# Loading q with four tokens to a partition, and its decay always at the cast, in a retention and Wave-MLP kernel

## The chip, the cores and the metric

The kernel runs on one core of one Trainium2 chip. The metric is the device time of one execution in microseconds (us), the median of several runs.

## What is computed

Inputs q, k and v are float32 of 4 batches, 8 heads, 768 tokens and 64 features. Each head h has a decay gamma_h = 1 - 2^(-5-h). The first stage is a linear recurrence over tokens t:

```python
state = gamma * state + outer(k[t], v[t])          # 64 x 64, for each batch and head
y[t]  = (1 / 8) * q[t] @ state
```

Its output, with the heads side by side, is x (4 x 768 x 512). The second stage is

```python
theta = x @ w_theta
yr = w_tok_r @ (x * cos(theta))                    # over tokens
yi = w_tok_i @ (x * sin(theta))
u = x + yr + yi
out = u + relu(u @ w_ch)                           # float32
```

## The kernel before

**Units.** The recurrence is cut into 24 units: 4 batches, 3 blocks of 256 tokens, 2 halves of 4 heads; unit n has half n mod 2. A unit loads 256 KB each of q, k and v. A partition holds two neighbouring tokens of 4 heads, so a load (`load_unit`, tokens `Lq`, `Lk`, `Lv`) is 128 partitions x 4 heads in rows of 2 x 64 floats, 512 bytes each. `kqf` tiles (16 buffers) take k and q, `vf` tiles (9) take v.

The decay over tokens is factored: v is multiplied by gamma^-t at its cast to bfloat16 (`cv`, table `vsc`), and q by gamma^t / 8. For q there are two ways, chosen unit by unit: either at the cast (`cqs`, table `qsc`), with a plain copy of the unit's output later (`XB`), or a plain cast (`cq`), and then the output, which has q's token in the free dimension, is multiplied by the table `qx` when it is copied out of PSUM (`XA`, DVE alone). `qx` is 128 x 4 x 768 floats, made by eight exponentials on ACT (`const8`, `const9`) from the positions that `constA` makes on POOL.

Then for a unit: `ck` casts k; `Tk`, `Tq` transpose k and q on PE and `E` copies them to `kqT` (or `Dk` does it by a DMA transpose on SP); `ST` adds k x v to the state in PSUM, `S0`, `S1` keep it in float32 and `SB` copies it in bfloat16 to block-diagonal tiles; `A` makes the scores `at_ps` and `m` multiplies them by the causal mask; `I` (state) and `Y` (scores x v) give the unit's output in PSUM; `XA` or `XB` copies it to `xT`, where the tokens lie in order.

**Chunks.** 128 tokens with all heads are a chunk C (24 in all, 6 to a batch). `Tx` and `Ex` (or `Dx`, a DMA transpose) give x; `Hh` is x @ w_theta, `CN` its sine and cosine on ACT, `z` the product with x. `M.t.s` adds chunk s of the batch to output tile t with both token matrices; `u` adds x; `Tu`, `Eu` (or `Du`) transpose u; `O` is u @ w_ch; `f` applies relu and adds u, into one of 4 `ot` buffers; `SO` stores. `Mh`, `uh` and so on are the last tile in halves. `Pth`, `Pch`, `Pw` load the weights by POOL's queue; `Tw`, `Ew` transpose the token matrices; `Z` are products of zeros on PE, written to no output.

**Order.** A list, `ORDER`, written out by hand or by a planner, gives one sequence of tokens; each engine executes its own instructions in that order. A letter at the end of a token names the engine or queue: p POOL (GpSimd), v DVE (VectorE), a ACT (ScalarE), s SP's DMA queue. So a load with an `a` stands in ACT's stream between its copies. DMAs of SP and ACT use eight semaphores in turn.

Of the kernel before, what the change touches and what calls it, by code (L numbers as in the profile page):

```python
# [25 lines left out]
Tk.1 E.1.a Y.0 ST.1 XB.0.1.a cqs.2.v Z.34 S0.1.v S1.1 cv.2.p SB.1.0.a Pth Lq.3.s Z.18 XB.0.0.v Tq.2  # L26
A.1 SB.1.1.a ck.2.a Tk.2 const7 I.1 Z.23 m.1 Y.1 XB.1.0.a Lk.3.s E.2.v XB.1.1.v A.2 ck.3.p m.2 ST.2
S0.2.v S1.2 SB.2.1.a Z.11 cqs.3.p Tq.3 Lv.3.s Tx.0 Tk.3 Z.3 ck.4.p Lv.4.s Lk.5.s Lq.5.s Lv.5.s
Lq.6.s Lk.6.s Lv.6.s Lq.7.s E.3.a SB.2.0.v I.2 Y.2 XB.2.1.a Ex.0.a cv.3.v cq.4.p Tk.4 Lq.8.s A.3
ST.3 Lk.7.s S0.3.v SB.3.0.a S1.3 Lv.7.s Lk.8.s Tx.1 Tq.4 SB.3.1.p cv.4.p m.3 Pw.1.0 XB.2.0.a Ex.1.a  # L30
I.3 Lv.8.s cq.5.a Y.3 E.4.a Pw.0.0 ST.4 Hh.0 ck.5.a cv.5.v CN.0.1 A.4 CN.0.0 S0.4.v Tq.5 Hh.1 Tk.5
XB.3.0.v SB.4.0.p XB.3.1.v SB.4.1.a Pw.0.1 Hh.2 m.4 E.5.v I.4 Y.4 ST.5 ck.6.a Tk.6 Tx.2 cq.6.a
CN.1.1 CN.1.0 XA.4.1 A.5 XA.4.0 m.5 Lq.9.s Ex.2.v S0.5.v z.0.p Tq.6 E.6.a CN.2.0 cv.6.p Hh.3
SB.5.0.v Tx.3 Tw.1.0 z.1.v SB.5.1.a Ew.1.0.v Ex.3.a CN.2.1 A.6 I.5 Y.5 ST.6 XA.5.0 z.2.v Tw.0.0
CN.3.0 Tx.4 CN.3.1 Ew.0.0.v S0.6.v XA.5.1 Ex.4.v Hh.4 CN.4.0 CN.4.1 Tw.0.1 M.0.1 Pw.1.1 z.3.v M.0.0
Tw.0.2 Pw.1.2 Ew.0.2.a SB.6.1.a Hh.5 z.4.p SB.6.0.p Lk.9.a M.0.3 ck.7.p cqs.7.p M.0.2 CN.5.1 CN.5.0
cq.8.a m.6 Ew.0.1.v Tw.1.1 Tw.1.2 Ew.1.1.v Lv.9.s M.0.4 M.1.0 Tx.5 Ew.1.2.v M.1.1 S1.6 Tk.7 M.1.4
Pch Ex.5.v cv.7.p z.5.v Tq.8 Tq.7 M.1.2 M.0.5 I.6 Y.6 ST.7 E.7.v ck.8.a A.7 u.0 S0.7.v m.7 XA.6.1
SB.7.1.a M.1.5 M.1.3 XA.6.0 Tw.1.3 M.2.5 Pw.0.2 M.2.3 u.1 S1.7 Tk.8 M.2.1 M.2.0 SB.7.0.v Ew.1.3.a
Tu.0 I.7 cv.8.p E.8.a cv.9.p Y.7 ST.8 A.8 cqs.9.v ck.9.v M.2.4 Du.1 Lk.10.s Eu.0.a XB.7.1.a XB.7.0.v  # L40
S0.8.v SB.8.0.v M.2.2 Tx.6 Tq.9 Tk.9 Lv.10.a cv.10.p ck.10.p Lq.10.s S1.8 u.2 m.8 O.0 E.9.a SB.8.1.a
Hh.6 Tw.1.4 I.8 Y.8 A.9 CN.6.0 Du.2 Lq.14.s CN.6.1 Ex.6.v f.0 ST.9 Tw.0.3 Hh.7 Ew.1.4.v Ew.0.3.a
S0.9.v Tw.0.4 M.3.0 Tw.1.5 CN.7.0 CN.7.1 M.3.2 Dx.7 M.3.1 M.3.5 M.3.3 Lv.12.s Lk.12.s Ew.1.5.v
XA.8.1 Ew.0.4.v Lq.12.s M.3.4 u.3 S1.9 Tw.0.5 Tk.10 M.4.5 cqs.10.p XA.8.0 m.9 M.4.3 Tq.10 SB.9.1.a
SB.9.0.a I.9 O.2 Lq.11.s Lk.11.s E.10.a Lk.15.s Ew.0.5.v Lk.14.s Y.9 ST.10 A.10 z.7.p Lv.11.s
# [24 lines left out]
u.12 A.20 Dk.21 XA.19.1 S0.20.v XA.19.0 ck.22.a cq.22.a SB.20.1.p cv.22.p M.14.3 M.14.5 M.14.1  # L70
M.14.4 M.14.2 M.14.0 SB.20.0.p u.13 m.20 S1.20 Hh.19 I.20 Y.20 SO.10.s Lq.23.s Lk.23.s cv.21.v u.14
A.21 ST.21 CN.19.0 CN.19.1 S0.21.v M.15.3 M.15.5 S1.21 m.21 XA.20.1 Hh.18 CN.18.1 CN.18.0 Dx.18
Dk.22 ck.23.a M.15.4 M.15.2 SB.21.0.p M.15.1 M.15.0 SB.21.1.v Lv.23.s Du.12 Dx.19 XA.20.0 O.9 f.9
I.21 Y.21 A.22 ST.22 M.16.1 cqs.23.p u.15 m.22 S0.22.v z.18.p z.19.p M.16.5 SB.22.0.p M.16.4 O.12
M.16.0 SO.8.a M.16.2 M.16.3 SB.22.1.p XB.21.0.a XB.21.1.a SO.11.s Du.14 cv.23.p Dk.23 f.12 Du.13
Dx.20 Dx.21 Hh.21 u.16 I.22 A.23 Y.22 ST.23 CN.21.0 CN.21.1 Hh.20 CN.20.1 S0.23.v XA.22.1 XA.22.0
SB.23.0.a M.17.1 M.17.3 CN.20.0 M.17.0 SB.23.1.p I.23 M.17.2 m.23 Y.23 O.13 M.17.4 z.21.v M.17.5
Mh.0.1 Mh.0.3 XB.23.1.v f.13 Hh.23 u.17 XB.23.0.a SO.13.a CN.23.1 Du.16 Hh.22 z.20.v CN.22.1 Mh.0.2
M.19.3 Dx.23 CN.23.0 Dx.22 Mh.0.0 M.21.1 M.19.1 z.23.p CN.22.0 SO.6.a Du.17 M.18.1 O.16 M.21.2
M.19.2 M.19.0 M.18.3 f.16 SO.9.a M.18.5 z.22.p M.18.2 O.17 M.19.4 M.18.0 Mh.0.4 M.18.4 f.17 u.18  # L80
Du.15 SO.12.s O.15 M.19.5 f.15 u.19 SO.16.s M.22.2 M.22.1 O.14 Mh.1.3 SO.15.a Mh.0.5 uh.0 f.14
M.22.0 M.21.5 M.22.3 M.22.5 Du.19 M.21.4 SO.17.s M.22.4 Du.18 M.21.0 O.19 Mh.1.0 Mh.1.2 M.21.3
M.20.2 Mh.1.4 u.22 O.18 f.19 M.20.0 M.20.1 Tuh.0 u.21 Du.22 Du.21 f.18 M.20.3 Euh.0 M.20.4 Mh.1.1
M.20.5 u.20 O.22 Mh.1.5 uh.1 f.22 Tu.20 SO.14.a SO.19.s Eu.20.a O.21 SO.18.a Tuh.1 Euh.1 f.21 O.20
f.20 Oh.0 Oh.1 SO.21.a SO.22.s SO.20.s fh.1 SOh.1 fh.0 SOh.0 Z.31
# [14 lines left out]
def kernel(  # L100
# [53 lines left out]
    def load_unit(name, src, n, e):  # L154
        b, i, h = unit(n)
        t = io.tile([P, HU, 2, D], FT, name="vf" if name == "vf" else "kqf", bufs=9 if name == "vf" else 16)
        queues[e].dma_start(
            out=t.rearrange("p h a d -> p h (a d)"),
            in_=src[b, h * HU:(h + 1) * HU, i * 2 * P:(i + 1) * 2 * P, :].rearrange(
                "h (p a) d -> p h (a d)", a=2))  # L160
        raw[name, n] = t
# [3 lines left out]

    def Lq(n, e):
        load_unit("qf", q, n, e)
# [35 lines left out]
    def const2():  # L203
# [4 lines left out]
        for h in range(H):  # L208
# [6 lines left out]
        nc.gpsimd.memset(K["zerob"], 0.0)  # L215
        arg = const.tile([P, nI * 2, H], FT, name="arg")
        nc.vector.tensor_mul(arg, _bcast_last(posn.rearrange("p i a -> p (i a)"), H),
                             _bcast_mid(lg, nI * 2))
# [415 lines left out]
```

## Time and profile before

| | |
|---|---|
| runs | median 168.77 us of 3 (168.33 to 169.25) |
| profiled execution | 168.7 us, span 166.9 us, granted PE clock 0.999 |
| busy, share of span | PE 92%, DVE 68%, ACT 47%, POOL 46% |
| DMA | 34.93 MB in 69,062 packets, mean 209 GB/s |
| first real transpose on PE | 7.46 us |
| scores (A) of units 0 to 5 start | 8.87, 12.44, 14.79, 18.52, 23.63, 27.59 us |
| loads, median time from issue to landing | q 5.0, k 5.2, v 5.8 us (SP's queue) |

Times are us, those of single instructions ns. PE is TensorE and PEld its weight loads, which overlap; the DMA slices are tenths of the 16 engines' time. A group's row gives line, engine, operation, tiles, count, busy us and mean ns, then the idle time of the engine just before and what ended it. A row of the waits gives who waited for whom, total us, times, and the longest. L numbers are lines of the kernel before, and in the changed kernel they are a few lines off.

### The profile page before, as it was taken

How to read it: one execution, taken by the hardware profiler on the slowest of the kernel's cores; microseconds unless marked ns; L12 is line 12 of the kernel's file. 1: busy time of each engine (PE TensorE's matmuls, PEld its weight loads, DVE VectorE, ACT ScalarE, POOL GpSimd, SP SyncE). 2: the span in 40 equal slices, each digit the busy share in tenths (PEclk: the TensorE clock that was granted, in tenths of full speed). 3: DMA queues.
4: the chain of work that ended last, by engine and by line, in shares of the span. 5: the costliest groups of instructions: out<-in, count | busy, mean ns of one | idle time of the engine just before them, and what ended most of it. 6: DMA issues, size and time to landing. Idle time of an engine off the chain costs nothing.

```text
span 166.9 us, 4887 instructions
## 1 busy us (share of the span) xinstructions
PE 153.7 (92%) x2001; PEld 86.8 (52%) x2030; DVE 114.0 (68%) x210; ACT 78.7 (47%) x141; POOL 76.6 (46%) x110
## 2 busy tenths in 40 slices
PE   5997779998999999999999999969999999999992
PEld 2455546655666556654555555435545544454550
DVE  3298657989994896994779895659868561254462
ACT  4965879981558345763333735822151426000020
POOL 7957369179206642630217699910459303600000
PEclk9999999999999999999999999999999999999999
DMA  4999999999999998949999995999899539414355
GB/s 121 297 290 244 280 282 265 259 227 251 195 197 224 296 184 203 312 102 266 298 301 191 173 245 146 260 215 232 150 216 162 119 64 247 159 61 127 88 211 208
DMA packets 69062, 34.93 MB, mean 209 GB/s; under 512 B 26416, under 2 KB 66096, under 8 KB 69040
## 3 DMA queue, kind: packets, MB, share of 16 engines
q1 hardware_dynamic: 56032, 23.73, 66.9%
q10 hardware_dynamic: 10320, 7.47, 15.5%
q0 software_dynamic: 2688, 3.41, 12.1%
q8 instruction: 16, 0.26, 0.7%
q14 instruction: 6, 0.05, 0.1%
HBM read 25.69 MB, written 6.29 MB: 192 GB/s over the span
## 4 chain that ended last, share of the span: by engine, by line
PE 75%; DMA 11%; ACT 5%; DVE 4%; issue 2%; POOL 2%; DVEq 0%; SPq 0%; POOLq 0%; ACTq 0%
PE y_ps L509 34%; PE o_ps L536 11%; PE th_ps L469 10%; DMA kqf<-in_k_dram 4%; PE r_ps L423 4%; DMA kqf<-in_q_dram 3%; DMA out_dram<-ot 3%; ACT qx L233 3%; PE at_ps L346 3%; PE w_ps L491 3%; PE r_ps L411 2%; PE kq_ps L316 2%; PE y_ps L561 2%; PE x_ps L455 1%; PE r_ps L373 1%
## 5 line engine op out<-in xcount | busy, mean ns | idle before, releaser
L509 PE MATMUL y_ps<-z,wtr 128*128 128x512 bf16 x131 | 49.8, 380 | 2.2 <-DVE ot L542 1.2
L509 PE MATMUL y_ps<-z,wti 128*128 128x512 bf16 x131 | 49.7, 379 | 1.0 <-issue 1.0
L483 POOL TENSOR_TENSOR z<-cs,x_sb 128x1024 bf16<-128x1024 bf16 x12 | 25.4, 2122 | 17.6 <-ACT cs L476 9.8
L355 DVE TENSOR_TENSOR at<-at_ps,mask 128x1024 bf16<-128x1024 f32 x24 | 29.2, 1216 | 0.6 <-PE at_ps L346 0.5
L308 POOL TENSOR_TENSOR vb<-vf,vsc 128x512 bf16<-128x512 f32 x18 | 18.8, 1047 | 21.3 <-DMA vf<-in_v_dram 20.9
L542 DVE SCALAR_TENSOR_TENSOR ot<-o_ps,u 128x512 f32<-128x512 f32 x23 | 15.9, 689 | 15.3 <-PE o_ps L536 12.1
L469 PE MATMUL th_ps<-wth,xT 128*128 128x512 bf16 x88 | 23.9, 380 | 0.5
L516 DVE TENSOR_TENSOR u<-y_ps,x_sb 128x512 bf16<-128x512 f32 x23 | 15.8, 688 | 11.5 <-PE y_ps L509 11.3
L536 PE MATMUL o_ps<-wch,uT 128*128 128x512 bf16 x88 | 23.2, 380 | 0.4 <-issue 0.2
L476 ACT ACTIVATE cs<-th_ps,zerob 128x512 bf16<-128x512 f32 x24 | 16.4, 685 | 13.0 <-PE th_ps L469 8.5
L476 ACT ACTIVATE cs<-th_ps,halfpi 128x512 bf16<-128x512 f32 x24 | 16.3, 685 | 12.9 <-issue 6.8
L139 POOL CAST sbd<-s 64x256 bf16<-64x256 f32 (+1 forms) x21 | 8.9, 423 | 26.9 <-DVE s L391 24.8
L509 PEld LDWEIGHTS <-wti 128*128 128x128 bf16 x138 | 13.5, 98 | 14.2 <-issue 2.5
L509 PEld LDWEIGHTS <-wtr 128*128 128x128 bf16 x138 | 13.4, 97 | 12.8
L137 ACT COPY kqT<-kq_ps 128x1024 bf16<-128x1024 bf16 x11 | 11.1, 1012 | 8.7 <-PE kq_ps L316 8.7
L137 ACT CAST kqb<-kqf 128x512 bf16<-128x512 f32 x17 | 10.3, 619 | 7.7 <-DMA kqf<-in_k_dram 6.0
L469 PEld LDWEIGHTS <-xT 128*128 128x128 bf16 x96 | 8.8, 98 | 8.3
L536 PEld LDWEIGHTS <-uT 128*128 128x128 bf16 x92 | 8.4, 98 | 8.6
L316 PE MATMUL kq_ps<-ident,kqb 128*128 128x128 bf16 x120 | 11.0, 220 | 0.5 <-ACT kqb L137 0.2
L278 PE MATMUL zz<-zero 128*128 128x512 bf16 x27 | 9.3, 477 | 2.0 <-DVE zero L192 1.9
L137 ACT CAST sbd<-s 64x256 bf16<-64x256 f32 (+1 forms) x19 | 6.9, 363 | 8.7 <-DVE s L139 4.0
L423 PE MATMUL r_ps<-at,vb 64*64 64x128 bf16 x384 | 10.0, 221 | 1.0 <-DVE at L355 1.0
(77 smaller groups left out, 207.0 us busy)
## 6 DMA issues: line engine op xcount, KB each, us to landing
vf<-in_v_dram SPq DMA_DIRECT2D x20, 256.0 KB, 5.8
kqf<-in_k_dram SPq DMA_DIRECT2D x19, 256.0 KB, 5.2
kqf<-in_q_dram SPq DMA_DIRECT2D x17, 256.0 KB, 5.0
out_dram<-ot ACTq DMA_DIRECT2D x12, 256.0 KB, 2.9
out_dram<-ot SPq DMA_DIRECT2D x11, 256.0 KB, 3.1
kqf<-in_q_dram ACTq DMA_DIRECT2D x7, 256.0 KB, 5.4
kqf<-in_k_dram ACTq DMA_DIRECT2D x5, 256.0 KB, 4.8
vf<-in_v_dram ACTq DMA_DIRECT2D x4, 256.0 KB, 5.3
```

The costliest lines, as they stand in the source:

```text
L137: nc.scalar.copy(dst, src)
L308: engines[e].tensor_mul(in_blocks(vb), by_token(raw["vf", n]), _bcast_last(K["vsc"][:, i, :, h * HU:(h + 1) * HU], D))
L316: nc.tensor.transpose(st["kq_ps", n][:, 4 * w + x, :], st["kqb", n][:, w, x * P:(x + 1) * P], K["ident"])
L355: nc.vector.tensor_mul(at.rearrange("p g j a t -> p (g j) (a t)"), st["at_ps", n].rearrange("p g j a t -> p (g j) (a t)"), _bcast_mid(K["m ...
L423: nc.tensor.matmul(st["R", n + 1][c][g * D:(g + 1) * D, j * P:(j + 1) * P], st["vb", n][rows, lo:lo + D], st["at", n][rows, g, j, a, :], s ...
L469: nc.tensor.matmul(th_ps, st["xT", C][:, j, :], K["wth"][:, j, :], start=(j == 0), stop=(j == 3))
L476: nc.scalar.activation(st["cs", C][:, w, :], st["th_ps", C], AF.Sin, bias=K["zerob" if w else "halfpi"], scale=1.0)
L483: engines[e].tensor_mul(st["z", b][:, c], st["cs", C], _bcast_mid(x_of(C), 2))
L509: nc.tensor.matmul(st["y", t], K["wT"][r][:, s0, t0 * P:(t0 + 1) * P], st["z", b][:, s0, r, :], start=(done == 0 and r == 0), stop=(done = ...
L516: nc.vector.tensor_add(st["u", t], st["y", t], st["x", b][:, t0, :])
L536: nc.tensor.matmul(o_ps, st["uT", t][:, j, :], K["wch"][:, j, :], start=(j == 0), stop=(j == nD - 1))
L542: nc.vector.scalar_tensor_tensor(st["ot", t], st["o", t], 0.0, st["u", t], ALU.max, ALU.add)
```

## The change

- q of a unit is loaded by two DMAs, `Lq` and `Lr`, of 128 KB each. A partition now holds four neighbouring tokens of two heads: partition j x 64 + p has tokens 4p to 4p+3 of heads 2j + g, where g is the DMA. Rows in memory are 4 x 64 floats, 1,024 bytes.
- q's decay is always applied at the cast. `cq`, `XA`, the table `qx`, `constA`, `const8` and `const9` are gone; all outputs of units are plain copies `XB`. The table `qsc` is laid out for the new partitions, from `posq` and `lgq`.
- k and v still hold two tokens to a partition, so q's columns come in another order: scores and state products read q's transpose in four runs of 32 columns instead of two of 64 (`qT`), the mask is made for it, and `XB` writes in steps that undo it.
- Buffers: kqf 16 to 18, vf 9 to 10, xT 4 to 5, uT 3 to 4, ot 4 to 6.
- `ORDER` is new throughout. By count: DMA transposes 41 for 37 (`Dx` 15 for 12, `Du` 17 for 16); z on DVE 17 for 12, on POOL 7 for 12; v's casts on DVE 14 for 6; q's casts 13 on DVE and 11 on POOL; `XB` 34 on ACT and 14 on DVE; loads on ACT's queue 30 for 16.

```diff
-const2 Lv.0.s const1 const6.v Z.29 Z.2 const5 Z.38 Lk.0.a const3 Z.35 Z.8 Lq.0.s Lv.1.s Z.28 constA
-const4 Lq.1.a cqs.0.v const9 Lk.1.s cv.0.p Z.39 const8 ck.0.p Tk.0 Tq.0 ck.1.a E.0.v Lq.4.a ST.0
-Lk.4.a Z.15 A.0 cqs.1.p Tq.1 Lq.2.s S0.0.v SB.0.1.v Lk.2.s SB.0.0.p cv.1.p Lv.2.s S1.0 I.0 Z.27 m.0
...
+const1 const6.v Z.34 Z.18 Z.23 Z.29 Z.35 Lr.0.a Z.3 Lq.0.s Z.39 Z.8 Z.27 Lr.1.s Lr.2.a Lq.1.s Lk.2.a
+Lk.0.s const2 const3 cqs.0.p Lk.1.a Lk.3.a Lv.0.s cv.0.v ck.1.a ck.0.v Lr.4.s cqs.1.p const5 Lv.1.s
+Lv.2.s Lr.3.s const4 Tq.0 Tk.0 ST.0 const7 ck.2.a E.0.a cv.1.p Tq.1 Z.2 Tk.1 E.1.a A.0 m.0 Lv.4.s
+Lk.4.s Lq.2.s Lq.5.a S0.0.a Lv.3.s Z.31 Lk.5.s cv.2.p S1.0 A.1 Lq.3.a ck.3.p ck.4.v m.1 SB.0.1.a
...
-        t = io.tile([P, HU, 2, D], FT, name="vf" if name == "vf" else "kqf", bufs=9 if name == "vf" else 16)
+        t = io.tile([P, HU, 2, D], FT, name="vf" if name == "vf" else "kqf", bufs=10 if name == "vf" else 18)
...
+    def q_load(n, g, e):
+        b, i, h = unit(n)
+        if ("qf", n) not in raw:
+            raw["qf", n] = io.tile([P, 2, 4, D], FT, name="kqf", bufs=18)
+        queues[e].dma_start(
+            out=raw["qf", n][:, g].rearrange("p a d -> p (a d)"),
+            in_=q[b, h * HU:(h + 1) * HU, i * 2 * P:(i + 1) * 2 * P, :].rearrange(
+                "(j g) (p a) d -> g j p (a d)", g=2, a=4)[g])
...
+        posq = const.tile([P, nI, 4], FT, name="posq")
+        lgq = const.tile([P, 2, 2], FT, name="lgq")
+        for j in range(2):
+            rows = slice(j * D, (j + 1) * D)
+            nc.gpsimd.iota(posq[rows], pattern=[[2 * P, nI], [1, 4]], base=1, channel_multiplier=4,
+                           allow_small_or_imprecise_dtypes=True)
+            for h in range(2):
+                for g in range(2):
+                    nc.vector.memset(lgq[rows, h, g:g + 1], math.log(gammas[h * HU + 2 * j + g]))
...
-    def decay(lo, hi):
-        for x in range(H // 2):
-            nc.scalar.activation(K["qx"][:, x, lo:hi], K["pos"][:, lo:hi], AF.Exp,
-                                 bias=K["lscale"], scale=K["lgp"][:, x:x + 1])
...
+    def qT(n, rows, j, c):
+        lo = j * D + c * D // 2
+        return st["kqT", n][rows, 1].rearrange("p a j t -> p (a j) t")[:, :, lo:lo + D // 2]
...
-    def cq(n, e):
-        copy(e, in_blocks(kqb_of(n)[:, 1]), by_token(raw["qf", n]))
...
-        engines[e].tensor_mul(in_blocks(kqb_of(n)[:, 1]), by_token(raw["qf", n]),
-                              _bcast_last(K["qsc"][:, i, :, h * HU:(h + 1) * HU], D))
+        engines[e].tensor_mul(q_blocks(kqb_of(n)[:, 1]), q_by_token(raw["qf", n]),
+                              _bcast_last(K["qsc"][:, i, :, h], D))
...
-                                         kqT[rows, 1, :, j, cols],
+                                         qT(n, rows, j, c),
...
-            st["xT", C] = work.tile([P, 4, P], BF, name="xT", bufs=4)
-        return (st["xT", C][:, 2 * h:2 * h + 2].rearrange("p j (t a) -> p j t a", a=2),
-                st["R", n + 1][c][:, :2 * P].rearrange("p (j a t) -> p j t a", j=2, a=2))
+            st["xT", C] = work.tile([P, 4, P], BF, name="xT", bufs=5)
+        return (st["xT", C][:, 2 * h:2 * h + 2].rearrange("p j (t a) -> p j t a", a=4),
+                st["R", n + 1][c][:, :2 * P].rearrange("p (j a t) -> p j t a", j=2, a=4))
...
-    def XA(n, c):
-        _, i, h = unit(n)
-        nc.vector.tensor_mul(
-            *out_of(n, c),
-            K["qx"][:, 2 * h:2 * h + 2, (2 * i + c) * P:(2 * i + c + 1) * P].rearrange(
-                "p j (t a) -> p j t a", a=2))
...
-        st["uT", t] = work.tile([P, nD, P], BF, name="uT", bufs=3)
+        st["uT", t] = work.tile([P, nD, P], BF, name="uT", bufs=4)
...
-        st["ot", t] = work.tile([P, dm], FT, name="ot", bufs=4)
+        st["ot", t] = work.tile([P, dm], FT, name="ot", bufs=6)
```

More of the change, by code (lines that the diff above doesn't have):

```diff
@@ L28 @@
[L28 to L33, printed above, removed]
@@ L219, in const2 @@
         K["arg"] = arg
-    def constA():
-        pos = big.tile([P, S], FT, name="pos", tag="z")
-        nc.gpsimd.iota(pos, pattern=[[1, S]], base=1, channel_multiplier=0,
-                       allow_small_or_imprecise_dtypes=True)
-        K["pos"] = pos
-        K["lgp"] = const.tile([P, H // 2], FT, name="lgp")
-        for h in range(H):
-            nc.gpsimd.memset(K["lgp"][(h % 2) * D:(h % 2 + 1) * D, h // 2:h // 2 + 1],
-                             math.log(gammas[h]))
-    def decay(lo, hi):
-        for x in range(H // 2):
-            nc.scalar.activation(K["qx"][:, x, lo:hi], K["pos"][:, lo:hi], AF.Exp,
-                                 bias=K["lscale"], scale=K["lgp"][:, x:x + 1])
     def const3():
-        K["qsc"] = const.tile([P, nI, 2, H], FT, name="qsc")
+        K["qsc"] = const.tile([P, nI, 4, 2, 2], FT, name="qsc")
         K["vsc"] = const.tile([P, nI, 2, H], FT, name="vsc")
-        for t, bias, sc in ((K["qsc"], K["lscale"], 1.0), (K["vsc"], K["zerob"], -1.0)):
-            nc.scalar.activation(t.rearrange("p i a h -> p (i a) h"), K["arg"], AF.Exp,
-                                 bias=bias, scale=sc)
-        K["qx"] = const.tile([P, H // 2, S], FT, name="qx")
-    def const8():
-        decay(0, 2 * P)
-    def const9():
-        decay(2 * P, S)
+        nc.scalar.activation(K["qsc"].rearrange("p i a h g -> p (i a) (h g)"), K["argq"], AF.Exp,
+                             bias=K["lscale"], scale=1.0)
+        nc.scalar.activation(K["vsc"].rearrange("p i a h -> p (i a) h"), K["arg"], AF.Exp,
+                             bias=K["zerob"], scale=-1.0)
     def const7():
@@ L259, in const5 @@
     def const5():
-        mask = const.tile([P, 2, 2, D], BF, name="mask")
+        mask = const.tile([P, 2, 4, D // 2], BF, name="mask")
         nc.gpsimd.memset(mask, 1.0)
@@ L411, in I @@
                 nc.tensor.matmul(r[c][:, j * P:(j + 1) * P], sbd_of(n)[:, c, j, :],
-                                 st["kqT", n][:, 1, :, j, c * D:(c + 1) * D],
+                                 qT(n, slice(0, P), j, c),
                                  start=(j == 0), stop=False, skip_group_check=True)
@@ L525, in Eu @@
     def Eu(t, e):
-        st["uT", t] = work.tile([P, nD, P], BF, name="uT", bufs=3)
+        st["uT", t] = work.tile([P, nD, P], BF, name="uT", bufs=4)
         copy(e, st["uT", t], st["u_ps", t])
     def Du(t):
-        st["uT", t] = work.tile([P, nD, P], BF, name="uT", bufs=3)
+        st["uT", t] = work.tile([P, nD, P], BF, name="uT", bufs=4)
         nc.sync.dma_start_transpose(out=st["uT", t], in_=st["u", t])
@@ L558, in Mh @@
                 st["u", last] = work.tile([P, dm], BF, name="u", bufs=4)
-                st["uT", last] = work.tile([P, nD, P], BF, name="uT", bufs=3)
+                st["uT", last] = work.tile([P, nD, P], BF, name="uT", bufs=4)
         for r in range(2):
```

129 lines of the change are left out of this document (73 added, 56 removed).

## The prediction

> **What bounds the kernel now.** I read the page first: engines, slices, chain.
>
> ```profile
> span 166.9 us, 4887 instructions
> PE 153.7 (92%) x2001; PEld 86.8 (52%) x2030; DVE 114.0 (68%) x210; ACT 78.7 (47%) x141; POOL 76.6 (46%) x110
> DMA  4999999999999998949999995999899539414355
> PE 75%; DMA 11%; ACT 5%; DVE 4%; issue 2%; POOL 2%; DVEq 0%; SPq 0%; POOLq 0%; ACTq 0%
> ```
>
> PE carries the time and DMA is full for the first half. Next the windows, to see where PE's idle time lies (the first pairs are the stretch, its length, and PE's busy time).
>
> ```profile
> 15.00:20.00 5.00, 4.25 (x111) 3.08 (x101) 3.37 (x9) 2.86 (x7) 1.62 (x4) 1.00 1.17 244
> 20.00:25.00 5.00, 3.39 (x63) 2.06 (x65) 3.09 (x6) 3.54 (x7) 3.19 (x5) 1.00 1.20 283
> 25.00:160.00 135.00, 130.43 (x1658) 73.44 (x1681) 95.92 (x173) 59.80 (x108) 59.94 (x61) 1.00 0.95 202
> 160.00:167.00 7.00, 3.78 (x27) 2.15 (x25) 3.16 (x6) 0.96 (x2) 0.00 (x0) 0.98 0.53 190
> ```
>
> From 25 to 160 us PE idles 4.6 us in 135. Before 25 us it is busy 19.4 us, but 9.3 us of that are products of zeros (group zz), so the head gives about 10 us of wanted work in 25: it costs 15 us, the middle 4.6, the tail 3.2. Anything that wins must win in the head. The chain of waits, in order of time (start, length, what), says what holds the head:
>
> ```profile
> 3.95 4.89 ACT qx L233 x8
> ...
> 9.25 6.63 DMA kqf<-in_k_dram
> ...
> 15.90 0.37 SPq L157
> ...
> 16.31 5.65 DMA kqf<-in_q_dram
> ...
> 22.04 0.62 ACT kqb L137
> 22.66 0.92 ACT kqT L137
> ...
> 23.63 0.42 PE at_ps L346 x16
> ```
>
> ACT builds the decay table qx for 4.9 us. Behind it stand its two loads of unit 4 (issued at 8.8 and 9.3, landed at 14.2 and 15.9). DMAs of SP and ACT take eight semaphores in turn and each waits for the DMA that held its semaphore; so SP, which holds nearly all loads, stands too:
>
> ```profile
> SPq L157 <- DMA kqf<-in_q_dram: 4.5, 1, 4.5
> ```
>
> Unit 5's q is therefore issued at 16.31, lands at 22.0, and ACT, waiting to cast it, has unit 4's kqT copy behind it. From 25 us on only one wait on the chain is long: f waits for one of four ot buffers.
>
> ```profile
> 104.87 5.60 DMA out_dram<-ot
> 110.56 0.70 DVE ot L542
> 111.30 4.05 PE y_ps L509 x18
> ```
>
> The waits price it: DVE 3.1 us, PE 1.24 us.
>
> **Part 1, q's rows.** 24 x 512 packets of 512 bytes become 24 x 256 of 1,024. In the trace's packet records a 512-byte packet takes 32.8 ns in the mean (median 29), a 1,024-byte one 48 ns (128 of them, the last stores). Over 16 engines a 256 KB load goes from 512 x 32.8 / 16 = 1.05 us to 256 x 48 / 16 = 0.77 us: 0.28 us a unit (0.16 by the medians). Units 0 to 5 have 18 loads: 1.9 (first packet) + 18 x 1.05 + 2.0 for the 512 KB of wth (two loads' worth) = 22.8, and unit 5's v did land at 22.8. With the new rows 12 x 1.05 + 6 x 0.77 gives 21.1, 1.7 us sooner (1.0 by the medians). The Trainium skill, "DMA: Bandwidth & Descriptors", section Specifications, gives 512 bytes as the smallest transfer at line rate, so by it the new rows are worth 0 and the supply stays at 22.8. The packet records here disagree (64 against 47 ns per KB), though the 1,024-byte ones come from a quiet time.
>
> Over the whole run q saves 25.2 - 18.5 = 6.7 us of DMA (3.8 by medians). Four more DMA transposes (41 for 37), 512 packets of 256 bytes at 25.7 ns each, give 3.3 back. So the middle is as full as before. There are 24 more DMAs, 128 KB each, to issue: SP has 66 loads for 56 (its issues take about 0.5 us each), ACT 30 for 16 at 0.44. Two stores leave ACT: 12 more issues, 5.3 us, in its stream; SP gets 10 x 0.5 + 2 x 0.55 + 4 x 1.24 = 11 us. SP is idle enough; whoever stands behind a load on ACT is the second rival.
>
> **Part 2, decay at the cast.** Removed: 8 qx activations (4 x 0.801 + 4 x 0.585 = 5.5 us busy), the 0.78 us iota and 8 memsets on POOL, 22 products with qx on DVE, 11 plain casts.
>
> ```profile
> L441 DVE TENSOR_TENSOR xT<-r_ps,qx 128x256 bf16<-128x256 f32 x22 | 8.7, 417 | 1.8 <-PE r_ps L373 1.8
> L302 POOL TENSOR_TENSOR kqb<-kqf,qsc 128x512 bf16<-128x512 f32 x7 | 7.2, 1039 | 0.0
> ```
>
> Added: 11 casts with the decay (0.68 on DVE, 1.04 on POOL) and 22 plain copies of xT (0.372 on ACT, 0.418 on DVE). Counting every step by the engine it now has: DVE -22 x 0.417 (products) +7 x 0.68 (q) +8 x 0.68 (v) +5 x 0.794 (z) +5 x 0.418 (xT) -5 x 0.418 -4 x 0.55 -5 x 0.287 (x_sb, wT, state) = +1.4, and 8 memsets and a product of constants, between 0.9 (POOL's 0.09 rows) and 2.4 (DVE's 0.27 memset); I take 1: 116.5. ACT -5.5 +17 x 0.372 +4 x 0.80 +2 x 0.586 +5 x 0.272 -7 x 0.619 -0.6 +0.4 = about 81. POOL -5 x 2.12 -8 x 1.05 -5 x 0.65 +4 x 1.04 and small ones: 57. No engine becomes the bound; DVE, at 70%, takes 15 more casts that wait for loads (33 for 18), POOL gives them up. PE loses 16 transposes of 128x128 (four take 0.22 us in the chain): -0.9 us, all on the path.
>
> The new patterns cost nothing, I take it: a moving operand in runs of 64 (L411, 219 ns) costs what one unbroken does (L316, 220), so runs of 32 should too. DVE's xT copies at 418 ns against a plain 128x128 state copy at 287 are about 1.0 ns an element, strided or not. If runs of 32 did cost, A and I (7 and 5 us on PE) would carry it: 0 to +1, taken 0.
>
> **Part 3, the new order, in the head.** Worked through by hand from rows. The first eight DMAs are five halves of q (0.385 each) and three full loads (1.05): 5.1 us of DMA, done by 7.0. ACT: three issues, table load, two scales until 4.2, issue of k for units 1 and 3, which share the engines with SP's next loads, so that k of unit 1 lands about 8.9 (two loads on) and is cast, the Sin table (1.6), cast of unit 2, kqT of units 0 and 1 at 12.7 and 13.7. POOL: two q casts, mask, identity ready at 8.0 (PE's first transpose; 7.46 before). So A.0 falls at 12.7 (8.87 before) and A.1 at 13.8 (12.44). The second half of unit 3's q, behind these on ACT and behind an issue and a state copy, is issued at 14.4 and lands about 16.7 (a 128 KB store took 1.8 us to land, half a microsecond for the company it has); its cast on POOL comes after unit 2's and v of 3 and ends about 18.2, ACT's kqT copy at 19.5 to 20: A.3 about 20 (18.52). Then the better supply tells: q and v of units 4 and 5 land by 18.6 and 20, A.4 about 22 (23.63), A.5 about 24 to 25.5 (27.59). PE work wanted ahead of A.5 is equal (12.1 us for 12.3, counts by rows), so PE is ahead by 2.1 to 3.6 there; I take 2.0, since the next weights on POOL's queue come no sooner. Bounds: -3.6 and +2.0 (rival B).
>
> **Part 4, buffers.** ot 4 to 6: the 1.24 us of PE at 110 us can go; 0 to -1.2, taken -0.8, since the next wait there is ACT's cast on a k load (3.2 us). kqf 18, vf 10, xT 5, uT 4: loads are asked for a little earlier; nothing further booked.
>
> **Part 5, new waits.** The 15 further casts on DVE hold m, u and f behind them. 18 cost DVE 5.1 us of waits before; 0.28 each makes 4 us more, of which PE sees little while it has M to do: 0 to +5, taken +1.2.
>
> Sum: 168.7 (span 166.9 and 1.8 around it; the median of the runs is 168.77) - 2.0 - 0.9 - 0.8 + 1.2 = 166.2.
>
> **Rivals.** A, the rows buy nothing: under load the 1,024-byte packet takes twice the 512-byte one. Then 1.7 of the head's 2.0 goes: 167.9. For it: no 1,024-byte load is in the trace. Against: the stores' 2,048 bytes take 91 ns, less than twice the 48. The Trainium skill's rule above is this rival, and so far the packet records speak against it.
>
> B, slower: ACT's queue in the head. Behind the wait for unit 1's k stand a table load, two kqT copies and then the loads of q for units 5 and 3; SP's loads of units 6 and 7 take the semaphores of just these two. It decides if unit 3's q lands after about 18.5: then A.3 falls past 21.5, kqT of unit 4 follows it on ACT, and SP stands as it did at 9 to 15.9 us. The head then loses 2.0 instead of gaining: 170.2. For it: ACT stood just so in the head before. Against: the qx block is gone, and 2 us of slack are left.
>
> C, slower: DVE at its casts. If the 15 wait as POOL's do (21.8 us over 37, 0.59 each: 9 us), and PE sees over half, the term is +5: 170.0. For it: POOL could wait unseen, DVE can't. Against: by the order, loads stand as far ahead or further.
>
> **Numbers.** Forecast 0.50, A 0.14, B 0.20, C 0.16. Half a per cent, 0.84 us, is about what a measurement here can tell from no change (the three runs spread 0.9). Faster: 0.47 of the forecast, 0.04 of A. Within: 0.03, 0.10 of A, 0.02 of B, 0.01 of C. Slower: 0.18 of B, 0.15 of C. So 0.51, 0.16, 0.33. The range takes the head at its full 3.6 and the store wait at 1.2 with 0.8 of new waits (163.8) and on the other side B or C with 0.6 to 0.8 of the patterns' bound (170.8); 0.07 lies below, 0.13 above. The forecast's own range is 164.5 to 167.8.
>
> **What would show it.** Right: no qx row; about 6,144 packets fewer on the load queues; q's issues land sooner than 5.0 us; A.5 at 24 to 25.5; no long wait of f on out_dram; PE idle 25 to 160 near 4. Wrong: A.3 after 21.5 with ACT or SP waiting for q (B); DVE's casts of q and v with several microseconds of idle before them on in_q or in_v and PE waiting for at or z (C); a 1,024-byte packet at 60 ns or more (A).

## The result: 275.4 us, and two DMA engines of sixteen

After: median 275.41 us of 4 runs (274.81 to 277.34); before, on the same chip, 168.74 us of 4 runs (168.33 to 169.25). The ratio is 1.634, 95% interval 1.625 to 1.643. The forecast was 166.2 us. Some executions come out over 1.5% above their kernel's fastest: here and below a ratio leaves them out (two of four in `e9`, three of six in `e16`) and a median takes all, and the profiled executions of `e1`, `e5`, `e9` and `e16` are such, by 2 to 7 us.

The page of the profile after: span, engines, the slices of PE's granted clock and of DMA, and the chain.

```profile
span 275.6 us, 4891 instructions
...
PE 176.7 (64%) x1985; PEld 96.4 (35%) x2014; DVE 115.1 (42%) x208; ACT 79.0 (29%) x154; POOL 58.5 (21%) x89
...
PEclk9755955795597796897989559968997998899998
DMA  2426843373396692399441997999999998724264
...
DMA  38%; SPq 25%; PE 21%; issue 8%; ACT 2%; DVE 2%; POOL 1%; ACTq 1%; DVEq 0%; POOLq 0%
```

DVE, ACT and POOL are about as busy as the prediction summed (115, 79 and 58 us for 116.5, 81 and 57). Yet the chain is DMA and SP's queue, 63% together, and where everybody waits for loads the DMA engines are *less* busy than before: slices of 2 to 4 tenths where there were 9s. The windows of after say the same (stretch, length, then busy time and count of PE, PEld, DVE, ACT, POOL; PE's clock, DMA share, GB/s):

```profile
15.00:20.00 5.00, 0.00 (x0) 0.00 (x0) 0.00 (x0) 2.03 (x3) 0.00 (x0) 0.50 0.26 81
20.00:25.00 5.00, 1.01 (x12) 0.81 (x15) 1.14 (x2) 0.67 (x2) 3.50 (x8) 0.50 0.45 135
25.00:160.00 135.00, 75.56 (x1007) 45.76 (x1021) 49.98 (x86) 43.10 (x81) 32.96 (x40) 0.77 0.63 118
```

A share of 0.26 with work queued points at a few busy engines and many idle ones. The timeline of after shows what that does to the queues (start, length, what; in brackets the idle time before):

```profile
0.80 5.98 SPq L172 DMA_DIRECT2D kqf<-in_q_dram  x3
...
6.83 4.95 SPq L159 DMA_DIRECT2D kqf<-in_k_dram  x1
...
10.91 1.05 POOL L315 TENSOR_TENSOR kqb<-kqf,qsc 128x512 bf16<-128x512 f32 x1 [9.16 <-DMA kqf<-in_k_dram]
...
17.94 0.62 ACT L139 CAST kqb<-kqf 128x512 bf16<-128x512 f32 x1 [12.07 <-DMA kqf<-in_k_dram]
...
20.19 1.05 POOL L315 TENSOR_TENSOR kqb<-kqf,qsc 128x512 bf16<-128x512 f32 x1 [8.23 <-DMA kqf<-in_q_dram]
...
23.99 1.01 PE L329 MATMUL kq_ps<-ident,kqb 128*128 128x128 bf16 x8 [15.81 <-POOL ident masks.py:199]
```

SP needs 6 us to issue three loads of q and another 5 to issue one of k; in the timeline of before, an issue at the same place took half a microsecond:

```profile
1.33 0.49 SPq L157 DMA_DIRECT2D kqf<-in_q_dram  x1
...
2.41 0.51 SPq L157 DMA_DIRECT2D kqf<-in_k_dram  x1
```

The first cast of q ends at 12 us (it reads q; the releaser in brackets is inferred), the second starts at 20.2, and the identity, which stands behind it on POOL, lets PE begin at 24 instead of 7.5. The chain of after goes on like that, one long issue after the other:

```profile
2.29 17.76 DMA kqf<-in_q_dram
...
26.36 2.69 SPq L159
...
29.09 0.70 SPq L159
...
29.84 2.72 SPq L172
...
32.60 5.52 SPq L172
```

Why so few engines? The trace's landing records count them. Of the DMAs on SP's and ACT's eight semaphores, a load of 256 KB leaves 16 records, one for each engine. After, there are 1,968 records: 114 other DMAs (48 loads of k and v, 41 transposes, 25 stores) make 16 x 114 = 1,824, and 144 are left, three for each of the 48 loads of q: one right at the issue (for the first load at 2.13 us) and two landings (10.65 and 10.75). (In the kernel `e5` below, with the same 162 DMAs, there are 2,591, sixteen for each but one.) So two engines carry a load of q, and the record at the issue would be the other fourteen at once. The packet records show the number by themselves. The two queues' packets of 4 bytes number 2,736 in before, which is 16 for each of 97 loads and stores and 32 for each of 37 transposes. By this count after should have 3,248, as `e5` has; it has 2,576, and the 672 that are missing are 14 for each of the 48 loads of q. For unit 0's k, 14 engines landed by 14.8 us and the last two at 20.8: the two behind q.

The diff says why two. Taken as (j, p, row), the pattern of `q_load` in memory is 2 x 64 x 256, with j, the pair of heads, outermost. `load_unit` has 128 partitions outermost. The Trainium skill, "DMA: Bandwidth & Descriptors", section "Why a DMA increments its semaphore by 16 and not by 1", states it: the number of engines is the largest one up to 16 that divides the outermost sizes (other than 1) of both patterns, and for a DMA of SP or ACT the rest of the 16 is written to the semaphore at once. The trace agrees: one record at the issue, then two (it keeps the time of a step, not its size), and 14 packets fewer. The same page's "Rules for kernel authors" asks for an outermost size that is a multiple of 16, ideally the 128 partitions.

The size fits. A 1,024-byte packet took 49.6 ns in the mean after, and 64 packets of each of 48 loads go to each of the two engines: 48 x 64 x 0.0496 = 152 us. Their sixteenth of all other traffic is 125 us, by the data packets of before without q, and 3.3 for the four more transposes. That estimate gives the two engines 281 us of work, 2% over the span of 275.6; by it they were busy nearly throughout.

### The profile page after: what moved, and what is told of

Read it like the earlier page. It is cut to its first block, busy times and chain, and to the rows that moved or that the text cites. A ratio compares the mean times of both kernels' runs of the same rounds, so it can differ in the third digit from the quotient of the medians.

```text
span 275.6 us, 4891 instructions
## 1 busy us (share of the span) xinstructions
PE 176.7 (64%) x1985; PEld 96.4 (35%) x2014; DVE 115.1 (42%) x208; ACT 79.0 (29%) x154; POOL 58.5 (21%) x89
## 4 chain that ended last, share of the span: by engine, by line
DMA 38%; SPq 25%; PE 21%; issue 8%; ACT 2%; DVE 2%; POOL 1%; ACTq 1%; DVEq 0%; POOLq 0%
DMA kqf<-in_q_dram 21%; SPq L172 11%; SPq L159 11%; PE y_ps L515 9%; DMA vf<-in_v_dram 5%; PE o_ps L542 5%; DMA kqT<-kqb 4%; DMA kqf<-in_k_dram 3%; DMA out_dram<-ot 2%; PE th_ps L475 2%; SPq L345 2%; DMA uT<-u 2%; PE y_ps L567 1%; ACT cs L482 1%; SPq L468 1%
## 5 line engine op out<-in xcount | busy, mean ns | idle before, releaser
L515 PE MATMUL y_ps<-z,wtr 128*128 128x512 bf16 x133 | 53.9, 406 | 2.9 <-ACT cs L482 2.6
L542 PE MATMUL o_ps<-wch,uT 128*128 128x512 bf16 x86 | 27.7, 437 | 11.9 <-DVE ot L548 4.3
L315 POOL TENSOR_TENSOR kqb<-kqf,qsc 128x512 bf16<-128x512 f32 x11 | 11.5, 1047 | 87.9 <-DMA kqf<-in_q_dram 51.1
L329 PEld LDWEIGHTS <-kqb 128*128 128x128 bf16 x120 | 9.6, 113 | 53.2 <-issue 24.1
L321 DVE TENSOR_TENSOR vb<-vf,vsc 128x512 bf16<-128x512 f32 x14 | 9.8, 711 | 32.1 <-DMA vf<-in_v_dram 32.1
L482 ACT ACTIVATE cs<-th_ps,halfpi 128x512 bf16<-128x512 f32 x24 | 16.2, 686 | 21.5 <-PE th_ps L475 10.1
L139 ACT CAST xT<-r_ps 128x256 bf16<-128x256 f32 x34 | 12.4, 373 | 31.3 <-PE r_ps L386 13.6
L489 DVE TENSOR_TENSOR z<-cs,x_sb 128x1024 bf16<-128x1024 bf16 x17 | 11.8, 706 | 17.6 <-ACT x_sb L139 11.8
L139 ACT CAST kqb<-kqf 128x512 bf16<-128x512 f32 x10 | 6.2, 616 | 41.3 <-DMA kqf<-in_k_dram 32.7
L386 PE MATMUL r_ps<-vb,kqb 64*64 64x64 bf16 x384 | 8.1, 207 | 14.8 <-DVE vb L321 12.1
L542 PEld LDWEIGHTS <-uT 128*128 128x128 bf16 x92 | 9.3, 108 | 21.5 <-issue 8.8
L489 POOL TENSOR_TENSOR z<-cs,x_sb 128x1024 bf16<-128x1024 bf16 x7 | 15.0, 2149 | 7.3 <-ACT cs L482 5.2
```

Of the source, the lines that this page charges most:

```text
L139: nc.scalar.copy(dst, src)
L329: nc.tensor.transpose(st["kq_ps", n][:, 4 * w + x, :], st["kqb", n][:, w, x * P:(x + 1) * P], K["ident"])
L482: nc.scalar.activation(st["cs", C][:, w, :], st["th_ps", C], AF.Sin, bias=K["zerob" if w else "halfpi"], scale=1.0)
L489: engines[e].tensor_mul(st["z", b][:, c], st["cs", C], _bcast_mid(x_of(C), 2))
L515: nc.tensor.matmul(st["y", t], K["wT"][r][:, s0, t0 * P:(t0 + 1) * P], st["z", b][:, s0, r, :], start=(done == 0 and r == 0), stop=(done = ...
L542: nc.tensor.matmul(o_ps, st["uT", t][:, j, :], K["wch"][:, j, :], start=(j == 0), stop=(j == nD - 1))
```

## Experiments

**1. How many engines carry q: 2, 4, 8, 16.** Two kernels of the new order with other patterns in memory (tiles, sizes and counts of instructions stay):

```diff
-            in_=q[...].rearrange("(j g) (p a) d -> g j p (a d)", g=2, a=4)[g])
+            in_=bass.AP(..., ap=[[S * D, 4], [4 * D, 32], [1, 4 * D]]))   # e2; e6: [[S * D, 8], [4 * D, 16], ...]
```

> The changed kernel with q's pattern given an outermost dimension of 4 (4 heads x 32 rows of 1,024 bytes for each DMA): the same bytes, rows, sizes and count, but q's tokens land in other partitions than the casts and scores take them for, so that the output is another. Theory 'engines': four engines carry q, 48 x 32 x 48 to 50 ns = 74 to 77 us each, beside 131 us of everything else: 195 to 215 us. Rivals 'small DMAs' and 'order': 275 as before the edit.

> The changed kernel with q's pattern given an outermost dimension of 8 (8 heads x 16 rows); the same bytes, rows, sizes and count, q's tokens in other partitions, so the output is another. Theory 'engines': eight engines carry 48 x 16 x 50 ns = 38 us of q beside 131 us of everything else, 169 us, so they are full as long as PE is: 170 to 185. Rival 'small DMAs' and 'order': 275 (k of 2 and 4 gave 275 and 214).

Measured: 214.32 us with 4 heads outermost and 184.95 with 8 (one run each), spans 212.6 and 183.2, both inside what the theory of the engines gave, at its upper end. The 4-byte packets are 576 and 384 short of 3,248: 12 and 8 for each load of q.

And two kernels of the old order, q in one DMA of 128 rows of 2,048 bytes, that differ in the outermost dimension alone:

```diff
+                        ap=[[S * D, 2], [8 * D, 64], [1, 8 * D]]))     # e3_before_k2
+                        ap=[[8 * D, P], [1, 8 * D]]))                  # e4_before_k16
```

> The kernel before, one edit: q of a unit is still one DMA of 256 KB, but its DRAM pattern has an outermost dimension of 2 (2 x 64 rows of 2,048 bytes); it takes other rows of q than the unit's, so that the output is another. Order, count and casts are those of before. Theory 'engines': two engines carry 24 x 64 x 91 ns = 140 us of q beside 128 us of the rest: 250 to 280 us. Rivals 'small DMAs' and 'order': 166 to 170, as before.

> Control for the run before: the kernel before with q as one DMA of 128 rows of 2,048 bytes that lie one behind the other (outermost dimension 128); it takes the same wrong rows' place as that run, so that the output is another. Theory 'engines' and both rivals: 164 to 169 us, with q's 25 us of DMA at 17; the row length alone costs nothing.

Measured: 262.58 and 167.74 us (one run each). The page of the first, then of the second:

```profile
span 260.9 us, 4887 instructions
...
PEclk9859555976988997775997997975997899999999
DMA  5143283836749999548439939799399999654445
...
DMA 53%; PE 21%; SPq 18%; POOL 3%; DVE 2%; issue 2%; ACT 0%; DVEq 0%; ACTq 0%
```

```profile
span 166.0 us, 4887 instructions
...
DMA  4999999999979979969999795999799528414575
```

The outermost dimension of one address pattern makes 95 us in the kernel before, with nothing of the change in it, and the profile looks like that of after: holes in DMA, SP and DMA on the chain, and PE's clock low as well (0.85). So the low clock, 0.82 after, comes along with the slow loads and is no cause of its own; what PE's longer busy time, 176.7 us for 153.7, adds to the 275 was not measured.

**2. The same rows on all engines.** `e1` splits q's loads by pairs of heads, each into one half of the partitions, with 64 partitions outermost.

```diff
-            out=raw["qf", n][:, g].rearrange("p a d -> p (a d)"),
-            in_=q[b, h * HU:(h + 1) * HU, ...].rearrange("(j g) (p a) d -> g j p (a d)", g=2, a=4)[g])
+            out=raw["qf", n][g * D:(g + 1) * D].rearrange("p g a d -> p g (a d)"),
+            in_=q[b, h * HU + 2 * g:h * HU + 2 * g + 2, ...].rearrange("g (p a) d -> p g (a d)", a=4))
```

> The changed kernel with one edit: the two DMAs of a unit's q are divided by partition half (each fills 64 partitions for both heads g) instead of by g, so that the outermost dimension of the DRAM pattern is 64 and not 2. Rows of 1,024 bytes, 128 KB a DMA, count, layout in the tile and order are the same. Theory 'engines' (a DMA is spread over as many of the 16 DMA engines as the outermost dimensions of both its patterns allow, here 2): the time falls to 164 to 170 us, since the two engines' 147 us of q packets (48 x 64 x 48 ns) become 18. Rival 'small DMAs' (48 DMAs of 128 KB on eight semaphores are what is slow): stays at 260 to 280. Rival 'order' (casts and loads stand where they block): above 200.

Measured: 181.18 us (6 runs), ratio 1.068, 1.064 to 1.072. The two rivals that left the time far above 200 fell; so did the theory's own 164 to 170. `e5` reaches all 128 partitions with each DMA, 64 outermost, and for that puts the pairs of heads into alternate partitions.

```diff
+                         ap=[[4 * D, D], [2 * S * D, 2], [1, 4 * D]]))
```

> The changed kernel, its q DMAs by g as they are (128 KB, all 128 partitions, 1,024-byte rows, same count and order), but with the DRAM pattern's dimensions p and j exchanged: outermost 64, so 16 engines. Partition 2p + j instead of 64j + p then holds a row, so casts and scores work on other tokens than they should and the output is another. Theory 'half of the partitions' (the run by partition half was 12 us above before because DMAs that fill only 64 partitions are slow: 72 to 75 ns for a 1,024-byte packet): packets at 48 to 52 ns and 165 to 170 us. Rival 'order and small DMAs' (the rest of the loss is the new order's, or that of 24 DMAs more): 178 to 182, as in that run.

Measured: 175.99 us (6 runs), ratio 1.037, 1.033 to 1.042, between what the two theories gave. By engines, then: 275.4, 214.3, 185.0, 176.0 us for 2, 4, 8, 16. 99 us of the 107 are the engines. What is left is 6 to 7 us over before, where the prediction had 2.5 us under it.

**3. What two DMAs for one, and halves of the partitions, cost.** The kernel before, its order and 512-byte rows kept, with q's load in two:

```diff
+        for x in range(2):          # e8: out=t[:, 2 * x:2 * x + 2], two heads each, all partitions
+            queues[e].dma_start(...)  # e7: out=t[x * D:(x + 1) * D], 64 partitions each, four heads
```

> The kernel before, q of a unit in two DMAs of 128 KB, each for all 128 partitions and 2 heads, 512-byte rows; all else as before. Theory 'half of the partitions': 168.5 to 171 us, packets near 33 ns. Rival 'small DMAs' (24 more DMAs on the eight semaphores and in the issue streams): 172 to 178, as with halves by partitions.

> The kernel before, q of a unit in two DMAs of 128 KB, each for 64 partitions and 4 heads, 512-byte rows; all else as before. Theory 'half of the partitions': packets of q at 37 ns or more for 32.8 and 171 to 178 us, clearly above the run with halves by heads. Rival 'small DMAs': the same time as with halves by heads. If both are at 169, neither costs anything in this order.

Measured: 173.08 us, ratio 1.021 (1.015 to 1.027), and 177.3 us, 1.048 (1.043 to 1.053). Two DMAs for one cost 3.5 us in the old order; scores of units 0 to 2 start as before (8.7, 12.3, 14.7), unit 3's at 21.8 instead of 18.5. Half partitions cost 4.6 more, by the ratios, with the same bytes, rows and number of DMAs, as `e1` is 5.2 over `e5`. So both theories hold in part. The 512-byte packets took 36 to 39 ns there, 31 to 37 in `e8`. The Trainium skill ("DMA: Bandwidth & Descriptors", "Rules for kernel authors") advises against splitting a transfer by halves of the partitions, since both use the same engines; the runs agree and add a price to it.

**4. Order, casts, loads, one at a time.** `e9` lays the order of before under `e5`; `e10` is before with the decay at each cast and the new buffers alone; `e11` is after's order with one DMA a unit, in rows of 2,048 bytes.

```diff
 e9, e10:  - constA const8 const9    cq.n.e -> cqs.n.e (ACT's five to DVE)    XA.n.c -> XB.n.c.v
 e9:       Lq.n.e -> Lq.n.e Lr.n.e
 e11:      Lq: ap=[[8 * D, P], [1, 8 * D]], Lr: nothing
```

> The kernel after with q spread over 16 engines and all 128 partitions (176.0 us, which is 6.8 over before), and with the order of before laid back under it: each load of q becomes its two halves on the same queue at the same place, each plain cast of q a cast with the decay on the same engine (ACT's five go to DVE), each product with qx a plain copy on DVE. Its output is that of the kernel with all partitions (pairs of heads mixed by the layout). Three theories for the 6.8 us. If the new order's head makes them (ACT's queue, rival B): about 169 to 171. If the two small DMAs a unit make them: 172 to 174, as in the kernel before with two DMAs for one (3.9 over). If the casts with the decay and the layout do: 175 to 177 again.

> The kernel before with Parts 2 and 4 alone: q's rows and its one DMA as before, order as before, but every q takes its decay at its cast (ACT's five casts of q go to DVE), the table qx with its iota, memsets and activations is gone, the 22 products with qx are plain copies on DVE, and there are 6 ot, 18 kqf, 10 vf, 5 xT, 4 uT buffers. By the prediction's terms without its order: ot -0.8, and the head without qx, which held ACT for 4.9 us: 0 to -2.5, so 165.5 to 168. By the theory that the casts cost (DVE's waits): 170 to 172.

> The kernel after in its own order, with all of a unit's q in one DMA of 128 rows of 2,048 bytes, one to a partition, at the place of the first half's load (the second half issues nothing). Other tokens of q land in each partition, so other sums come out; work and order are the kernel's. If the two small DMAs make the 6.8 us: 168 to 171. If the new order's head does: 173 to 176, with A of unit 3 still past 24 us.

Measured: `e9` 1.020 (1.015 to 1.026), 172.6 us by that ratio's two executions, as the theory of the two small DMAs had it; `e10` 170.51 us, 1.008 (1.005 to 1.011), a small loss, inside what the theory of the casts gave; `e11` 176.63 us, 1.039 (1.032 to 1.045), just over what the theory of the order gave, with unit 3's scores at 24.7. So each of two things costs alone, the second DMA 2 to 3.5 us in the old order, the new order some 6.5 us with one DMA, and together (`e5`) they cost no more than the order does.

Where the order loses is read from the start of the scores of unit n, less the wanted PE work that its order puts ahead of it (without the zeros; each token at its duration in the rows of before). This lag is what PE has idled, or run slowly, until then (one profiled execution each; in that of `e5` the later columns are too high by up to 3 us):

```
lag, us, at the scores of unit    0     3     5     7     12    23
before                            8.1  12.8  15.3  16.7  16.3  16.4
e10, decay at each cast           7.4  12.7  16.2  18.0  17.6  17.4
e11, new order, one DMA          13.3  18.5  18.8  20.2  21.7  23.1
e5, new order, two DMAs          13.6  22.1  22.7  24.1  23.8  25.3
e13, e11 with zeros              13.0  17.5  18.0  19.9  19.5  24.3
e17, e11 with ACT reordered      10.7  17.1  17.4  18.7  20.4  21.9
```

In `e11` PE is 5 us later than before at the first scores, still 3.5 at unit 5, and 6.7 at unit 23. The timeline of ACT in `e11` shows the first part:

```profile
10.75 0.62 ACT L139 CAST kqb<-kqf 128x512 bf16<-128x512 f32 x1 [7.39 <-DMA kqf<-in_k_dram]
11.38 1.28 ACT L255 ACT_TABLE_LOAD   x1
...
12.88 0.60 ACT L139 CAST kqb<-kqf 128x512 bf16<-128x512 f32 x1
...
13.39 1.92 ACT L139 COPY kqT<-kq_ps 128x1024 bf16<-128x1024 bf16 x2
```

Unit 0's transposes had ended by 9.7 us, but its copy stands behind a wait for unit 1's k, a table load and a cast.

**5. The half clock.** In `e11` PE's granted clock stood at 0.50, half speed, from 13.3 to 20 us, in `e5` and `e10` too for a part of the head. `e12`, `e13` and `e14` put zeros into PE's waits there (16, 10 and 5 tokens `Z`), on `e5`, `e11` and `e10`.

```diff
-Tq.0 Tk.0 ... Tk.1 E.1.a A.0 ... SB.0.0.a I.0
+Z.0 Z.0 Tq.0 Tk.0 ... Z.0 Tk.1 E.1.a Z.0 Z.0 Z.0 Z.0 Z.0 Z.0 A.0 ... SB.0.0.a Z.0 I.0     (e13; the others alike)
```

> The kernel after with q on 16 engines and all partitions (176.0 us), with 16 more products of zeros on PE where it waits in the head: 6 before the first transpose, 3 after it, 1 and 3 before the products I of units 0 and 1, 1 and 2 behind them. There PE's clock was 0.50 at 12 to 15 and at 22 to 29 us, with 8.8 us of PE busy, so 4.4 us of PE's work were lost. If the half clock makes the loss: the clock stays at 1.00 and the time falls by 2 to 4.4 us, to 171.5 to 174. If the waits themselves make it: A of unit 5 stays at 34.8 and the time at 175 to 177.

> The same with all of q in one DMA a unit (176.6 us; other tokens to a partition): 10 more products of zeros, 2 before the first transpose, 1 before unit 1's, 6 before A of unit 0, 1 before I of unit 0. PE's clock was 0.50 from 13.3 to 20 us with 5.6 us of PE busy, so 2.8 lost. If the half clock makes the loss: 173.5 to 175. If not: 176 to 177.

> The kernel before with the decay at every cast, no table and the new buffers (170.5 us), with 5 more products of zeros in PE's waits between 17.4 and 21.8 us. PE's clock was 0.50 from 22.5 to 25.3 us, 1.4 us lost. If the half clock makes its 1.3 us over the kernel before: 168.5 to 169.5. If DVE's casts or ACT's waits do: 170 to 171.

The windows of `e11`, then of `e13` (stretch, length, PE busy and count, clock, DMA share, GB/s):

```profile
10.00:15.00 5.00, 1.65 (x26) 0.83 1.17 310
15.00:20.00 5.00, 4.57 (x68) 0.50 1.14 296
20.00:25.00 5.00, 4.43 (x127) 0.99 1.14 288
```

```profile
10.00:15.00 5.00, 5.00 (x58) 1.00 1.17 314
15.00:20.00 5.00, 3.32 (x81) 1.00 1.14 293
20.00:25.00 5.00, 4.78 (x116) 1.00 1.14 290
```

In these stretches the clock is whole, yet the times are 175.07 (1.034, 1.027 to 1.040), 175.66 (1.033, 1.026 to 1.040) and 169.88 us (1.003, 1.001 to 1.005): gains of 0.4, 0.6 and 0.5%, all short of what the theory gave, the first two within their intervals. What PE does faster it waits for a little later, at 15 to 20 us already: it idles 1.7 us there, where `e11` idled 0.4. By the starts of the scores `e13` is 1.0 us ahead of `e11` at unit 3 and 0.3 at unit 7.

The clock did not stay whole, though. The profiled executions lost it again further on, that of `e12` from 36.6 to 40.0 us, that of `e13` from 127.3 to 130.7, where 3.4 us at half speed cost 1.7 us and `e13`'s lag passes that of `e11`; only `e14` kept it up to 167 us. So zeros in the head bought 0.7 to 1.0 us here, and how much a clock that stays whole throughout would be worth in the new order stays open.

**6. ACT's first instructions.** `e16` (on `e5`) and `e17` (on `e11`) load the Sin table in ACT's idle time and copy unit 0's kqT ahead of the two casts.

```diff
-const3 ... ck.1.a ck.0.v ... ST.0 const7 ck.2.a E.0.a
+const3 const7 ... ck.0.v ... ST.0 E.0.a ck.1.a ck.2.a
```

> The kernel after with q on 16 engines and all partitions (176.0 us), with ACT's first instructions in another order: the Sin table is loaded right after the two scales, while ACT waits, and unit 0's kqT copy stands ahead of the casts of units 1 and 2. Before, ACT waited 5.4 us for k of unit 1, then loaded the table for 1.6 us, cast unit 2 and only then copied kqT of unit 0, so that A of unit 0 started at 14.8. Now A of unit 0 should start at 11.5 to 12.5 and A of unit 1 by 14. If ACT's order makes the loss: A of unit 3 by 25.5 and the time at 172 to 174.5. If the supply of q does: A of unit 3 stays past 27.5 and the time at 175 to 177.

> The same edit of ACT's order with all of q in one DMA a unit (176.6 us; other tokens to a partition). If ACT's order makes the loss: A of unit 0 at 11.5 to 12.5, of unit 3 by 23, and 172.5 to 174.5. If the supply does: A of unit 3 at 24 to 25 as before and 175.5 to 177.

Measured: `e16` 175.11 us, ratio 1.021 (1.015 to 1.027) against 1.037 for `e5`, 2.7 us; by the medians, 175.1 against 176.0, it is 0.9. In its profiled execution, at half clock from 10.8 to 24.5 us, the first scores start at 14.0, not at 11.5 to 12.5, and unit 3's at 26.2, between both expectations. `e17` 176.18 us, 1.041 (1.035 to 1.046): nothing, though the first scores start at 11.9 instead of 14.4 and unit 5's 1.4 us sooner. So with two DMAs ACT's queue may be a part of the loss, which is not shown; with one, something later sets the time.

For that something `e11` shows two candidates, which no run was made for. First, a cast of k on DVE that took 2.23 us (median of the six: 0.46), with POOL's product z beside it nearly all the while; PE waited 1.0 us for it, and the lag rises by 1.6 at unit 11. The timelines of POOL and DVE in `e11`:

```profile
65.93 2.17 POOL L486 TENSOR_TENSOR z<-cs,x_sb 128x1024 bf16<-128x1024 bf16 x1
...
66.15 2.23 DVE L141 CAST kqb<-kqf 128x512 bf16<-128x512 f32 x1
```

The kept traces settle what it costs. In `e13`, with the same order, POOL waits longer for a load of v, its product starts only at 67.6 us, and the same cast, at 65.3, takes 0.43. From the scores of unit 10 to those of unit 11 it is 6.4 us in `e13`, and in `e5`, `e12` and `e16`, none of which has a cast of 2 us there; in `e11` and `e17`, which have one, it is 8.3 and 8.4. So the two instructions meeting cost 2 us in these two executions, and nothing in that of `e5`.

Second, a DMA transpose that came late, one of the 41 (PE's waits of `e11`, 112 to 127 us); the lag rises by 1.1 there, and what that costs in the end is not shown:

```profile
PE at_ps L356 <- DMA kqT<-kqb: 1.3, 1, 1.3
```

**7. One part that gains.** `e15` is before with one number changed:

```diff
-        st["ot", t] = work.tile([P, dm], FT, name="ot", bufs=4)
+        st["ot", t] = work.tile([P, dm], FT, name="ot", bufs=5)
```

> The kernel before with five ot buffers for four and nothing else. The wait of f for out_dram at 110 us cost PE 1.24 us. By the prediction's Part 4 (-0.8, 0 to -1.2): 167.8 to 169.0 where before takes 169. If the wait only moves on: 169.

Measured: 168.01 us (167.43 to 168.5, 5 runs), ratio 0.991 (0.988 to 0.994): a gain of 0.9%, small but clear of the spread, and inside the expectation. The windows of before, then of `e15`, where f had waited for a store (columns as in the windows of after):

```profile
100.00:120.00 20.00, 18.23 (x234) 9.39 (x236) 14.05 (x28) 7.93 (x15) 10.39 (x14) 1.00 0.98 205
```

```profile
100.00:120.00 20.00, 19.62 (x270) 10.38 (x272) 15.05 (x29) 8.80 (x16) 12.40 (x15) 1.00 1.02 204
```

PE is busy 1.4 us longer in that stretch, and no wait of DVE for out_dram is left.

## Why the prediction was wrong

- **Part 1, the step that failed.** "Over 16 engines a 256 KB load goes from 512 x 32.8 / 16 = 1.05 us to 256 x 48 / 16 = 0.77 us": it was never asked whether the new pattern still goes over 16. The count belongs to the pattern's outermost size, which the diff shows: j, two. With 2 in place of 16, and after's 49.6 ns, Part 1's own formula gives 256 x 49.6 ns / 2 = 6.3 us a unit, 152 us in all on two engines that have 128 us of other work. The runs showed 99 us for it (`e5` against after). No rival had it; all three lay within 4 us of the forecast.
- **Part 1, the packet.** 48 ns for 1,024 bytes came from a quiet time, as the text said. With q on all engines it was 62.5 ns in the mean of both queues in `e5` and 59.0 in `e12`, against 31.6 and 30.4 for 512 bytes in the same runs: nothing a byte is won. That is rival A, whose mark was 60 ns or more. The Trainium skill's line rate from 512 bytes on ("DMA: Bandwidth & Descriptors", Specifications) agrees here. It does not quite for 2,048 bytes, which took 99 ns in `e4` and `e11` (q's and the stores' together), less than four of the 512-byte packets there, 124 to 126.
- **Part 1, the issues.** 24 more DMAs were called free on SP. In the old order they cost 2.1 us (`e9` against `e10`, the new rows and layout included) to 3.5 us (`e8`).
- **Part 2, the decay at the cast.** The engines' sums hold. The step from sums to time did not: `e10` should have come out under before by Parts 2 and 4 and was 1.3 us over, while one more `ot` buffer alone gains 1.6. Zeros gave 0.8 us back; what the rest is stays open.
- **Part 3, the head.** -2.0 was forecast. In after itself the loads of q undo it: the first scores start at 27.1 us, unit 5's at 57.5. With 16 engines (`e5`) the first scores start at 14.8 (12.7 forecast), unit 3's at 28.4 (20), unit 5's at 34.8 (24 to 25.5). That meets rival B's mark, scores of unit 3 past 21.5 us. Its place, ACT's queue, is likely for two DMAs (`e16`) and not shown; with one DMA it moves starts, not the end (`e17`). Its price, 170.2 us, was too low by 5.
- **Part 4, buffers.** Right in kind, and half the size: -0.8 was taken, -1.6 measured with five `ot` buffers (1.0 to 2.1 by the interval). The other buffers were not tried alone.
- **Part 5, new waits.** They can't be judged in after, where DVE waits for loads as all do. In the new order with 16 engines PE's longest wait for a cast on DVE is 1.0 us in `e11` and 1.3 in `e5`; rival C, with 5 us, isn't borne out.

## What to carry to other kernels

Before costing a DMA, read the outermost size of both its patterns: a rearrangement that puts a 2 ahead of 64 partitions keeps the bytes, the rows and the tile and gives the transfer to two engines. In a profile it shows as loads that everybody waits for, a DMA share far below one, and issues of several microseconds on the queue. And test the parts of a bundle alone: here one more `ot` buffer gained, and the other parts that were tried, the second DMA, the decay at every cast and the order, each lost.

## What the runs showed of the hardware

- Two full engines hold up the other loads too, since each has its sixteenth on them (k of unit 0: 14 engines by 14.8 us, the last two at 20.8), and the issuing queue stands with them: 5 us for one issue.
- 48 loads of 128 KB into 64 partitions each cost the kernel 4.6 us (`e7` over `e8`) and 5.2 us (`e1` over `e5`) more than the same bytes in as many loads over 128 partitions.
- A cast on DVE with one input took 2.23 us beside a product on POOL (`e11`) and 0.43 without it (`e13`). The Trainium skill, "SBUF — State Buffer", has the two engines share a port pair that, for some of DVE's instructions, one of the two holds for a whole instruction; the two rows shown agree, ending within 0.3 us of each other.
- PE's clock fell to 0.50 at 22.1 us in `e10` after a stretch with no idle time over 0.6 us: from 19 to 22 us PE was busy 1.4 us of 3, transposes among them. The Trainium skill, "TensorE: Matmul & The Clock Gate", warns of idle gaps over some 3 us; here a half-busy stretch was enough, while before kept 1.00 at 3.1 us of 5 (19 to 24). The page also says that transposes do not count as busy time in the same way; no run here tried that.
